# A spectral layer and an MLP on one core: MLP parts in a fixed order on TensorE, a stage moved to a later stretch, constants split early

## The chip, the cores and the metric

The kernel runs on one core of a Trainium2 chip. A core has TensorE (PE: matmuls, with its weight loads shown apart as PEld), VectorE (DVE), ScalarE (ACT), GpSimd (POOL) and SyncE (SP, which only issues DMAs here). ACT issues some DMAs too. The metric is the device time of one execution in microseconds; less is better.

## The reference

An input `x` of 8 batches, 3008 rows and 256 columns goes through a Fourier transform along the rows, a complex linear map with a soft threshold, and the inverse transform. The 24064 resulting rows are the tokens of an MLP with 2048 hidden units.

```python
X = np.fft.rfft(x, axis=1)
Yr = Xr @ w_r - Xi @ w_i + b_r
Yi = Xr @ w_i + Xi @ w_r + b_i
Yr = np.sign(Yr) * np.maximum(np.abs(Yr) - lam, 0.0)      # Yi likewise, lam = 0.01
y = np.fft.irfft(Y, n=x.shape[1], axis=1)
h = y.reshape(B * S, D) @ w_in
out = np.maximum(0.01 * h, h) @ w_out
```

## The kernel before

**The transform** of length 3008 = 47 x 64 is done in stages, each a set of matmuls. `fwd(b)`, the first stage of batch b, loads `xin`, folds it on POOL (`fold`), splits it into a high and a low half on DVE (`split`), multiplies it with `fa` (PE, L78, `psf<-xz,fa`), copies the result on ACT (L256) and stores it to `u_dram`. `mid(b)`, the middle stage, takes 12 pairs of columns one after the other: it loads `u` from `u_dram` (SP, L321), multiplies with `fb` (`stage_b`, PE L335), splits the result into `eh` (ACT and DVE, L346 to L351), multiplies with `wr`, `wn` and `wd` (`proj`, PE L78), applies the threshold (DVE L382 to L384), splits again into `zh`, multiplies with `gb` (`stage_g`) and stores `v_dram`. `inverse` (PE L472) and `forms` make the tokens of a chunk of 512: `yh` and `yl`, the high and low halves of seven sums of blocks. Products are taken in high and low halves throughout, three matmuls for one product.

**The MLP** works on 47 chunks of tokens with 8 steps each, 376 steps in all. A step does two of the 16 blocks of hidden units as a 2 x 2 block product by seven products (a scheme of Strassen's kind). `moe_a` issues four of them, twelve matmuls of 256 columns (PE L84, `psh<-yh,win`), into two PSUM banks b1 and b2; then ACT copies a quarter out (`p1`, L534) and DVE makes three sums of 256 columns that read the banks: `u2` (L535), and two into `gf` (L537, L538). `moe_b` adds the other three products, nine matmuls, to the same quarters of the banks: first b1, then b2. Its results go through ACT (L548), DVE (L549, 512 columns) and ACT (L551) into `gf`, then through ACT into `gh` (L553, 1024 columns) and DVE into `gl = gf - gh` (L555, 1024 columns). `moe_o` multiplies `gh` and `gl` with `wout`, six matmuls of 512 columns (PE L568) for each half of the output, LAG = 2 steps later. There are four `psh` banks, so two steps are in flight.

**What sets the order.** The code is written as generators: `moe()` yields twice in each step, and at each yield a share of the other stages' work is taken from a `Stream`, in proportion to how far the MLP has come. The time of the MLP is cut into stretches by `read[b]`, the point at which batch b's tokens are first needed. In stretch `cur` the streams are `fwd(cur + 2)` and `mid(cur + 1)`. From this a scheduler in the framework fixes, for each engine, the order of the instructions before the program runs; it picks by priority and by what its own timing of the program says is ready. At run time each engine then takes its instructions in that order. `tc.issue_after(ins)` puts the instructions that are traced within it behind `ins`, on `ins`'s engine alone, and adds no wait.

`split_consts` splits six constants into halves (ACT casts the high half, DVE subtracts for the low half). It is called after `mid(0)` behind a DVE instruction of it.

Of the kernel before, what the change touches and what calls it, by code (L numbers as in the profile page):

```python
# [8 lines left out]
F32 = mybir.dt.float32  # L9
# [21 lines left out]
def spectral_mlp_kernel(  # L31
# [16 lines left out]
    nc = tc.nc  # L48
    NB = x.shape[0]
# [8 lines left out]
    CS = 512  # L58
    LAG = 2

    NPRE = 2
# [5 lines left out]
    sync, act, dve, pool = nc.sync, nc.scalar, nc.vector, nc.gpsimd  # L67

    def bank(tag, bufs):
        return ps.tile([P, 512], F32, name=tag, tag=tag, bufs=bufs)  # L70

    def products(dst, pairs):
# [5 lines left out]
            last = nc.tensor.matmul(dst, a, b, start=(i == 0), stop=(i == len(terms) - 1))  # L78
        return last

    def block(dst, l, r, start=False):

        for i, (a, b) in enumerate(((l[0], r[0]), (l[0], r[1]), (l[1], r[0]))):
            nc.tensor.matmul(dst, a, b, start=start and i == 0, stop=i == 2, skip_group_check=True)  # L84

    def flat(t):
        return t.rearrange("p a b -> p (a b)")
# [4 lines left out]
    def pair(name, shape):  # L92
        consts[name] = tuple(const.tile(shape, F32R, name=f"{name}_{p}") for p in ("hi", "lo"))
        return consts[name]
# [5 lines left out]
    def split_consts():  # L100
        for name in ("wr", "wd", "wn", "gb", "fa0", "fa1"):
            w = consts[name + "32"][0]
            hi, lo = pair(name, list(w.shape))
            act.copy(hi, w)
            dve.tensor_sub(lo, w, hi.bitcast(F32))
# [12 lines left out]
    def float64_parts(raw, a, q):  # L118


        wl, wh = raw[:, :, 0], raw[:, :, 1]
        u = a.bitcast(U32)
        act.mul(q, wl, 2.0 ** -52)
        act.activation(a, wh.bitcast(F32), AF.Abs, scale=2.0 ** 16)
        dve.tensor_scalar(a, a, F64_MIN * 2.0 ** 16, F64_MAX * 2.0 ** 16, ALU.max, ALU.min)
        dve.tensor_scalar(u, u, 4, 1, ALU.logical_shift_left, ALU.logical_shift_right)
        dve.scalar_tensor_tensor(u, wh, 0x80000000, u, ALU.bitwise_and, ALU.bitwise_or)
        dve.tensor_scalar(wl, u, 0xFF800000, None, ALU.bitwise_and)
        dve.tensor_mul(q, q, wl.bitcast(F32))


    made, converted = [], []


    NIN = DF // 4
# [13 lines left out]
    def convert_win(c):  # L149


        a, q, s = win_tmp
        float64_parts(win_raw[c], a, q)
        dve.tensor_add(a, a, q)
        a = a.rearrange("p (j q i m) -> p j q i m", j=NH, q=2, i=2)
        a11, a12, a21, a22 = (a[:, j, :, i] for i in range(2) for j in range(2))
        dve.tensor_add(s[:, 0], a21, a22)
        dve.tensor_sub(s[:, 2], a11, a21)
        dve.tensor_sub(s[:, 1], s[:, 0], a11)
        dve.tensor_sub(s[:, 3], a12, s[:, 1])  # L160
        hi, lo = (w[:, :, 2 * c:2 * c + 2] for w in consts["win"])
        for k, w in ((slice(0, 2), a[:, :, :, 0]), (2, a22), (slice(3, 7), s)):
            act.copy(hi[:, k], w)
            last = dve.tensor_sub(lo[:, k], w, hi[:, k].bitcast(F32))
        return last
# [37 lines left out]
    reads, written, turned, turning, thresholded = [], [], [], [], []  # L203
# [100 lines left out]
    def mid(b):  # L304
# [13 lines left out]
        def load(j):  # L318
            u = sb.tile([P, 2, D], F32, name="u", tag="u", bufs=3)
            for c in range(2):  # L320
                ld = sync.dma_start(u[c * N2:(c + 1) * N2], ud[c, 2 * j:2 * j + 2, :N2, :].rearrange("k n d -> n k d"))  # L321
                if b == 0:
                    reads.append(ld)
            u_t[j] = u
# [88 lines left out]

        for j in range(2):
            load(j)
        yield 0
        if b:
            for s in range(NPAIR):
                if s + 2 < NPAIR:
# [100 lines left out]
    def product(dst, ci, q, k, start=False):  # L520
        block(
            dst, tuple(w[:, AK[k - 1], q] for w in consts["win"]), tuple(y[:, BK[k - 1]] for y in y_t[ci]), start)

    def moe_a(ci, q):

        b1, b2 = bank("psh", 4), bank("psh", 4)
        lo, hi = slice(0, HT), slice(HT, NT)
        product(b1[:, lo], ci, q, 1, True)
        product(b1[:, hi], ci, q, 6)
        product(b2[:, hi], ci, q, 7, True)  # L530
        product(b2[:, lo], ci, q, 5)
        p1 = sb.tile([P, HT], F32, name="p1", tag="p1", bufs=1)
        u2 = sb.tile([P, HT], F32, name="u2", tag="u2")
        act.copy(p1, b1[:, lo])  # L534
        dve.tensor_add(u2, b1[:, hi], p1)  # L535
        g = sb.tile([P, 4, HT], F32, name="gf", tag="gf")
        dve.tensor_add(g[:, 3], b2[:, hi], u2)  # L537
        dve.tensor_add(g[:, 3], b2[:, lo], g[:, 3])  # L538
        h_t[ci, q] = (b1, b2, u2, g)

    def moe_b(ci, q):

        b1, b2, u2, g = h_t.pop((ci, q))
        lo, hi = slice(0, HT), slice(HT, NT)
        product(b1[:, lo], ci, q, 2)
        product(b2[:, lo], ci, q, 3)
        product(b2[:, hi], ci, q, 4)
        act.activation(g[:, 0], b1[:, lo], AF.Prelu, alpha=SLOPE)  # L548
        dve.tensor_add(  # L549
            g[:, 1:3], b2.rearrange("p (k n) -> p k n", k=2), u2.unsqueeze(1).broadcast_to([P, 2, HT]))  # L550
        act.activation(g[:, 1:4], g[:, 1:4], AF.Prelu, alpha=SLOPE)  # L551
        gh = sb.tile([P, 4, HT], F32R, name="gh", tag="gh")
        act.copy(gh, g)  # L553
        gl = sb.tile([P, 4, HT], F32R, name="gl", tag="gl")
        dve.tensor_sub(gl, g, gh.bitcast(F32))  # L555
        g_t[ci, q] = (gh, gl)

    def moe_o(ci, q, eh):
        gh, gl = (t.rearrange("p (i k) n -> p i (k n)", i=2) for t in g_t[ci, q])
        wh, wl = consts["wout"]  # L560
        if q == 0:
            o_t[ci, eh] = bank("pso", 2)
        po = o_t[ci, eh]
        s = slice(eh * P, (eh + 1) * P)
        for i in range(2):
            f = 2 * q + i
            for j, (a, r) in enumerate(((wh, gh), (wl, gh), (wh, gl))):
                nc.tensor.matmul(  # L568
                    po, a[:, f, s], r[:, i], start=(f == 0 and j == 0), stop=(f == NF - 1 and j == 2),
                )  # L570
        if q == NQ - 1:
            ob = sb.tile([P, NT], F32, name="ob", tag="y")
            act.copy(ob, po)
            sync.dma_start(out[s, ci * NT:(ci + 1) * NT], ob)

    steps = [(ci, q) for ci in range(nch) for q in range(NQ)]
# [22 lines left out]
    def moe():  # L599

        for i, (ci, q) in enumerate(steps):
            if q == 0:
                nxt = tokens(ci + 1) if ci + 1 < nch else iter(())
            moe_a(ci, q)
            if i >= LAG:
                moe_o(*steps[i - LAG], 0)
            next(nxt, None)
            yield ci + (q + 0.5) / NQ
            if i >= LAG:
                moe_o(*steps[i - LAG], 1)  # L610
            moe_b(ci, q)
            next(nxt, None)
            if q == NQ - 1:
                for _ in nxt:
                    pass
            yield ci + (q + 1) / NQ
        for s in steps[-LAG:]:
            for eh in range(NH):
                moe_o(*s, eh)

    class Stream:
        def __init__(self, gen, total):
# [13 lines left out]
    MID = NPAIR * (16 * P + 18 * D + 3 * CS)  # L636
    FWD = NS * 6 * D
# [33 lines left out]
    dve.tensor_sub(bz[32:33], brow[32:33], bz[32:33].bitcast(F32))  # L671
    act.mul(fa32[:, 2], fa32[:, 1], -1.0)
    convert_win(0)
    m0 = Stream(mid(0), MID)
    m0.to(0.001)
    for c in range(2, 4):
# [22 lines left out]
    for eh in range(NH):  # L699
        for p in due[0]:  # L700
            inverse(p, eh)
    with tc.issue_after(thresholded[-1].ins):
        split_consts()
    for _ in forms(0):
        pass
    next(wout)
    next(wout)


    mids = [Stream(mid(b), MID) for b in range(1, NB)]  # L710
    cur, streams = -1, ()
    for i, pos in enumerate(moe()):
        if i % 2 == 0 and len(converted) < NQ:
            with tc.issue_after(made[0].ins):
                next(wout, None)
        if i in (2, 4):
            with tc.issue_after(made[0].ins):
                next(fp.gen)
        while cur + 1 < NB - 1 and pos >= (read[cur + 1] if cur >= 0 else 0):
            for s in streams:  # L720
                s.finish()
            cur += 1
            streams = ([Stream(fwd(cur + NPRE), FWD)] if cur + NPRE < NB else []) + [mids[cur]]
        frac = (pos - read[cur]) / (read[cur + 1] - read[cur]) if cur + 1 < NB else 1
        if cur == 0:
            frac = max(0, frac - 0.2) * 1.25
        work = frac / 0.95 * sum(s.total for s in streams)
        with tc.issue_after(converted[-1].ins) if cur == 0 else nullcontext():
            for s in streams:
                s.to(work / s.total)  # L730
                work = max(0, work - s.total)
# [103 lines left out]
```

## Time and profile before

| | |
|---|---|
| median of 3 runs | 2608.39 us (2605.04 to 2613.94) |
| the profiled execution: time, span of its instructions | 2609.83 us, 2608.0 us |
| PE busy | 2543.3 us, 98% of the span, 16300 matmuls |
| PEld busy | 2283.9 us, 88% |
| DVE busy | 1884.8 us, 72% |
| ACT busy | 1654.5 us, 63% |
| POOL busy | 248.2 us, 10% |
| granted TensorE clock, mean | 0.991 |
| chain that ended last | PE 90%, DVE 3%, ACT 3%, DMA 1% |

Busy times are unions of the instructions' spans. Matmuls overlap, so what PE has room for is read from the distance between the starts of neighbouring matmuls, not from the duration of one. In the tables of stretches, each engine has its busy time and, in brackets, the number of its instructions.

### The profile page before, as it was taken

What the parts mean: (1) busy time and instruction counts of PE and PEld (TensorE: products, weight loads), DVE (VectorE), ACT (ScalarE), POOL (GpSimd) and SP (SyncE); (2) the same over time, 40 slices, a digit from 0 to 9 for tenths busy, and PEclk for the clock granted to TensorE, in tenths of its full rate; (3) what the DMA queues carried; (4) which work ended last, traced back from release to release, by engine and by line L of the source; (5) the groups of instructions that cost most, each with busy time, mean ns of one, the idle gap of its engine ahead of it and who ended that gap; (6) DMA issues with size and microseconds to landing.
All of it is one profiled execution on the core that took longest, in us unless ns stands there. A gap on an engine that the chain in (4) does not pass through costs nothing.

```text
span 2608.0 us, 42647 instructions
## 1 busy us (share of the span) xinstructions
PE 2543.3 (98%) x16300; PEld 2283.9 (88%) x16300; DVE 1884.8 (72%) x3403; ACT 1654.5 (63%) x3174; POOL 248.2 (10%) x180
## 2 busy tenths in 40 slices
PE   5899999999999999999999999999999999999999
PEld 3678887999989999899999999999999999989998
DVE  6697667777787777777777777777777767667665
ACT  4665665676656666567665766666666666655554
POOL 0002102100120001200021000211000000000000
PEclk8999999999999999999999999999999999999999
DMA  8634113211142112312123111231111111100000
GB/s 248 172 99 116 53 42 92 84 52 47 32 120 61 48 37 56 101 53 59 33 74 94 52 45 41 74 94 52 45 41 53 41 41 44 42 18 32 9 17 17
DMA packets 119914, 165.14 MB, mean 63 GB/s; under 512 B 13602, under 2 KB 69918, under 8 KB 119710
## 3 DMA queue, kind: packets, MB, share of 16 engines
q1 hardware_dynamic: 79120, 115.55, 14.5%
q10 hardware_dynamic: 40589, 46.87, 7.1%
q8 instruction: 128, 2.10, 0.3%
q14 instruction: 77, 0.62, 0.1%
HBM read 86.60 MB, written 75.76 MB: 62 GB/s over the span
## 4 chain that ended last, share of the span: by engine, by line
PE 90%; DVE 3%; ACT 3%; DMA 1%; issue 1%; ACTq 0%; SPq 0%; DVEq 0%
PE pso L568 38%; PE psh L84 34%; PE psf L78 11%; PE psf L472 3%; PE psf L335 3%; DVE gl L555 1%; ACT zf L392 0%; ACT gh L553 0%; ACT gf L551 0%; DMA u_dram<-xin 0%; DVE yl L498 0%; ACT zf L388 0%; DMA raw<-w_out_dram 0%; DVE gf L549 0%; ACTq L412 0%
## 5 line engine op out<-in xcount | busy, mean ns | idle before, releaser
L84 PE MATMUL psh<-yh,win_hi 128*128 128x256 f32 x2632 | 738.4, 285 | 8.1 <-ACT yh L497 4.1
L84 PE MATMUL psh<-yl,win_hi 128*128 128x256 f32 x2632 | 735.1, 281 | 0.0
L84 PE MATMUL psh<-yh,win_lo 128*128 128x256 f32 x2632 | 727.2, 280 | 0.0
L555 DVE TENSOR_TENSOR gl<-gf,gh 128x1024 fp32r<-128x1024 f32 x376 | 475.9, 1266 | 197.5 <-ACT gh L553 195.9
L568 PE MATMUL pso<-gh,wout_hi 128*128 128x512 f32 x1504 | 596.0, 396 | 1.9 <-ACT gh L553 1.8
L568 PE MATMUL pso<-gh,wout_lo 128*128 128x512 f32 x1504 | 591.3, 393 | 0.0
L568 PE MATMUL pso<-gl,wout_hi 128*128 128x512 f32 x1504 | 559.8, 396 | 2.7 <-DVE gl L555 2.4
L84 PEld LDWEIGHTS psh<-yh,win_hi 128*128 128x128 f32 x2632 | 494.3, 189 | 33.6 <-ACT yh L497 5.7
L84 PEld LDWEIGHTS psh<-yl,win_hi 128*128 128x128 f32 x2632 | 497.1, 189 | 25.8 <-issue 0.5
L84 PEld LDWEIGHTS psh<-yh,win_lo 128*128 128x128 f32 x2632 | 493.5, 189 | 4.0 <-issue 0.2
L551 ACT ACTIVATE gf<-gf 128x768 f32<-128x768 f32 x376 | 318.6, 848 | 216.3 <-DVE gf L549 211.3
L553 ACT CAST gh<-gf 128x1024 fp32r<-128x1024 f32 x376 | 395.5, 1052 | 16.5 <-ACT gf L551 10.5
L549 DVE TENSOR_TENSOR gf<-psh,u 128x512 f32<-128x512 f32 x376 | 258.9, 689 | 198.4 <-PE psh L84 196.6
L568 PEld LDWEIGHTS pso<-gl,wout_hi 128*128 128x128 f32 x1504 | 282.5, 188 | 60.7 <-DVE gl L555 7.9
L568 PEld LDWEIGHTS pso<-gh,wout_lo 128*128 128x128 f32 x1504 | 282.9, 188 | 45.1
L568 PEld LDWEIGHTS pso<-gh,wout_hi 128*128 128x128 f32 x1504 | 283.0, 188 | 41.2 <-ACT gh L553 3.0
L548 ACT ACTIVATE gf<-psh 128x256 f32<-128x256 f32 x376 | 144.4, 384 | 214.2 <-PE psh L84 193.0
L371 POOL TENSOR_TENSOR kb<-bias,kc 128x512 f32<-128x512 f32 x84 | 121.4, 1446 | 1468.3 <-ACT kc L368 1302.2
L534 ACT COPY p<-psh 128x256 f32<-128x256 f32 x376 | 139.5, 371 | 100.0 <-PE psh L84 82.2
L535 DVE TENSOR_TENSOR u<-psh,p 128x256 f32<-128x256 f32 x376 | 157.8, 420 | 60.8 <-ACT p L534 58.2
L537 DVE TENSOR_TENSOR gf<-psh,u 128x256 f32<-128x256 f32 x376 | 157.6, 420 | 22.3 <-PE psh L84 11.1
L538 DVE TENSOR_TENSOR gf<-psh,gf 128x256 f32<-128x256 f32 x376 | 158.0, 421 | 6.8
(134 smaller groups left out, 3290.9 us busy)
## 6 DMA issues: line engine op xcount, KB each, us to landing
u<-u_dram SPq DMA_DIRECT2D x192, 128.0 KB, 2.7
v_dram<-v ACTq DMA_DIRECT2D x192, 128.0 KB, 2.4
out_dram<-ob SPq DMA_DIRECT2D x94, 256.0 KB, 2.1
vin<-v_dram SPq DMA_DIRECT2D x96, 240.0 KB, 3.5
xin<-x_dram SPq DMA_DIRECT2D x90, 240.0 KB, 3.0
u_dram<-xin ACTq DMA_DIRECT2D x72, 240.0 KB, 2.4
u_dram<-xin SPq DMA_DIRECT2D x24, 240.0 KB, 4.6
raw<-w_out_dram SPq DMA_DIRECT2D x8, 512.0 KB, 4.9
```

The source lines that it names most:

```text
L78: last = nc.tensor.matmul(dst, a, b, start=(i == 0), stop=(i == len(terms) - 1))
L84: nc.tensor.matmul(dst, a, b, start=start and i == 0, stop=i == 2, skip_group_check=True)
L534: act.copy(p1, b1[:, lo])
L535: dve.tensor_add(u2, b1[:, hi], p1)
L537: dve.tensor_add(g[:, 3], b2[:, hi], u2)
L538: dve.tensor_add(g[:, 3], b2[:, lo], g[:, 3])
L548: act.activation(g[:, 0], b1[:, lo], AF.Prelu, alpha=SLOPE)
L549: dve.tensor_add(g[:, 1:3], b2.rearrange("p (k n) -> p k n", k=2), u2.unsqueeze(1).broadcast_to([P, 2, HT]))
L551: act.activation(g[:, 1:4], g[:, 1:4], AF.Prelu, alpha=SLOPE)
L553: act.copy(gh, g)
L555: dve.tensor_sub(gl, g, gh.bitcast(F32))
L568: nc.tensor.matmul(po, a[:, f, s], r[:, i], start=(f == 0 and j == 0), stop=(f == NF - 1 and j == 2),)
```

## The change

It has three parts.

1. `in_order` puts each part of the MLP on PE behind the last matmul of the part before. The order of the parts in a step is also another: it was first products, output half 0, output half 1, last products in the code (with the scheduler free to mix them); it is now first products (of step i), output half 0 (of step i - 2), last products (of step i), output half 1 (of step i - 2), and the scheduler can't mix them any more. Other stages' matmuls may still stand between them.
2. `fwd(b)` for b from 2 to 7 is taken in stretch b - 1, ahead of `mid(b)` in the same stretch, where it was taken in stretch b - 2 beside `mid(b - 1)`. The middle stage yields 6 * CS of work after its first loads, so that its first matmul comes about a step later in the order. The two last pieces of `fwd(1)` stand behind `gh` and `gl` of the first steps.
3. `split_consts` is called after the first stage of batch 0, with its ACT halves behind the last copy of that stage; its DVE halves are no longer behind `mid(0)`.

```diff
+    mlp = []
+    def in_order(part, *args):
+        with tc.issue_after(mlp[0].ins) if mlp else nullcontext():
+            part(*args)
...
-            nc.tensor.matmul(dst, a, b, start=start and i == 0, stop=i == 2, skip_group_check=True)
+            mlp[:] = [nc.tensor.matmul(dst, a, b, start=start and i == 0, stop=i == 2, skip_group_check=True)]
...
-        yield 0
+        yield 6 * CS if b else 0
...
-        dve.tensor_sub(gl, g, gh.bitcast(F32))
+        parted[:] = [cp, dve.tensor_sub(gl, g, gh.bitcast(F32))]
...
-            moe_a(ci, q)
+            in_order(moe_a, ci, q)
             if i >= LAG:
-                moe_o(*steps[i - LAG], 0)
+                in_order(moe_o, *steps[i - LAG], 0)
             next(nxt, None)
             yield ci + (q + 0.5) / NQ
+            in_order(moe_b, ci, q)
             if i >= LAG:
-                moe_o(*steps[i - LAG], 1)
-            moe_b(ci, q)
+                in_order(moe_o, *steps[i - LAG], 1)
...
+    with tc.issue_after(turned[0].ins):
+        split_consts()
...
-    with tc.issue_after(thresholded[-1].ins):
-        split_consts()
...
-    mids = [Stream(mid(b), MID) for b in range(1, NB)]
+    mids = [Stream(mid(b), MID + 6 * CS) for b in range(1, NB)]
...
-            with tc.issue_after(made[0].ins):
+            with tc.issue_after(parted[0].ins), tc.issue_after(parted[1].ins):
                 next(fp.gen)
...
-            streams = ([Stream(fwd(cur + NPRE), FWD)] if cur + NPRE < NB else []) + [mids[cur]]
+            streams = ([Stream(fwd(cur + 1), FWD + 4 * CS)] if cur else []) + [mids[cur]]
```

What stands where is seen best at the end of the program, where no other stage's work is left. The names carry buffer numbers; all lines of the changed kernel's MLP are 8 higher (L84 is L92, L568 is L576, L535 is L543, L537 and L538 are L545 and L546, L549 is L557, L555 is L563). First PE before, from the last of the first products of one step (banks `psh_28039` and `psh_28040`) on:

```order
L84 MATMUL psh_28040<-yh_27478,win_lo_187 128x256
L84 MATMUL psh_27991<-yh_27478,win_hi_186 128x256
L84 MATMUL psh_27991<-yl_27479,win_hi_186 128x256
L84 MATMUL psh_27991<-yh_27478,win_lo_187 128x256
L84 MATMUL psh_27991<-yh_27478,win_hi_186 128x256
L84 MATMUL psh_27991<-yl_27479,win_hi_186 128x256
L84 MATMUL psh_27991<-yh_27478,win_lo_187 128x256
L84 MATMUL psh_28039<-yh_27478,win_hi_186 128x256
L84 MATMUL psh_28039<-yl_27479,win_hi_186 128x256
L84 MATMUL psh_28039<-yh_27478,win_lo_187 128x256
L568 MATMUL pso_27813<-gh_27986,wout_hi_897 128x512
L568 MATMUL pso_27813<-gh_27986,wout_lo_898 128x512
```

Ten more matmuls of L568 follow before `psh_28040` is written again. The same banks on PE in the changed kernel:

```order
L92 MATMUL psh_28040<-yh_27478,win_lo_187 128x256
L576 MATMUL pso_27813<-gh_27980,wout_hi_897 128x512
L576 MATMUL pso_27813<-gh_27980,wout_lo_898 128x512
L576 MATMUL pso_27813<-gl_27982,wout_hi_897 128x512
L576 MATMUL pso_27813<-gh_27980,wout_hi_897 128x512
L576 MATMUL pso_27813<-gh_27980,wout_lo_898 128x512
L576 MATMUL pso_27813<-gl_27982,wout_hi_897 128x512
L92 MATMUL psh_28039<-yh_27478,win_hi_186 128x256
L92 MATMUL psh_28039<-yl_27479,win_hi_186 128x256
L92 MATMUL psh_28039<-yh_27478,win_lo_187 128x256
L92 MATMUL psh_28040<-yh_27478,win_hi_186 128x256
```

Before, six matmuls of 256 columns on `psh_27991`, three on `psh_28039` and twelve of 512 columns stand between the last first product and the return to `psh_28040`; now six of 512 and three of 256. DVE at the same place before (`gf_27959` and `gf_28008` are the results of two neighbouring steps, and `gl_27988` is made from `gf_27959`):

```order
L535 TENSOR_TENSOR u2_28005<-psh_27990,p1_28004 128x256
L549 TENSOR_TENSOR gf_27959<-psh_27942,u2_27956 128x512
L537 TENSOR_TENSOR gf_28008<-psh_27991,u2_28005 128x256
L538 TENSOR_TENSOR gf_28008<-psh_27991,gf_28008 128x256
L535 TENSOR_TENSOR u2_28054<-psh_28039,p1_28053 128x256
L555 TENSOR_TENSOR gl_27988<-gf_27959,gh_27986 128x1024
L537 TENSOR_TENSOR gf_28057<-psh_28040,u2_28054 128x256
L538 TENSOR_TENSOR gf_28057<-psh_28040,gf_28057 128x256
```

DVE now, the same two steps:

```order
L557 TENSOR_TENSOR gf_27959<-psh_27942,u2_27956 128x512
L563 TENSOR_TENSOR gl_27982<-gf_27959,gh_27980 128x1024
L543 TENSOR_TENSOR u2_28005<-psh_27990,p1_28004 128x256
L545 TENSOR_TENSOR gf_28008<-psh_27991,u2_28005 128x256
L546 TENSOR_TENSOR gf_28008<-psh_27991,gf_28008 128x256
L557 TENSOR_TENSOR gf_28008<-psh_27991,u2_28005 128x512
L563 TENSOR_TENSOR gl_28031<-gf_28008,gh_28029 128x1024
```

Before, `gl` of one step stood behind all three reads (L535, L537, L538) of the next step's banks; now it stands ahead of them. In the middle of the program, where other stages' work stands between, an example on DVE now, from `gl` of one step to the last read of the next step's banks:

```order
L563 TENSOR_TENSOR gl_13249<-gf_13207,gh_13247 128x1024
L509 TENSOR_TENSOR yt_13411<-yc_12722 128x256
L543 TENSOR_TENSOR u2_13275<-psh_13260,p1_13274 128x256
L484 TENSOR_TENSOR y_13376<-psf_13370,odd_13375 128x240
L486 TENSOR_TENSOR y_13376<-psf_13370,odd_13375 128x230
L545 TENSOR_TENSOR gf_13278<-psh_13261,u2_13275 128x256
L390 TENSOR_TENSOR t_13423<-psf_13382,kb_13297 128x512
L511 TENSOR_TENSOR yt_13411<-yc_12722,yt_13411 128x256
L512 TENSOR_TENSOR yc_12722<-yc_12722 128x256
L546 TENSOR_TENSOR gf_13278<-psh_13261,gf_13278 128x256
```

Six instructions of other stages stand between `gl` and L546 here; in the kernel before, L538 of the same numbered step follows L537 directly, with no other stage's work behind `gl`:

```order
L538 TENSOR_TENSOR gf_13399<-psh_13382,gf_13399 128x256
L555 TENSOR_TENSOR gl_13360<-gf_13312,gh_13358 128x1024
L535 TENSOR_TENSOR u2_13462<-psh_13447,p1_13461 128x256
L537 TENSOR_TENSOR gf_13465<-psh_13448,u2_13462 128x256
L538 TENSOR_TENSOR gf_13465<-psh_13448,gf_13465 128x256
```

That `gl` belongs to the step two before, not to the step just before.

More of the change, by code (lines that the diff above doesn't have):

```diff
@@ L129, in float64_parts @@
         dve.tensor_mul(q, q, wl.bitcast(F32))
-    made, converted = [], []
+    made, converted, parted = [], [], []
     NIN = DF // 4
@@ L552, in moe_b @@
         gh = sb.tile([P, 4, HT], F32R, name="gh", tag="gh")
-        act.copy(gh, g)
+        cp = act.copy(gh, g)
         gl = sb.tile([P, 4, HT], F32R, name="gl", tag="gl")
-        dve.tensor_sub(gl, g, gh.bitcast(F32))
+        parted[:] = [cp, dve.tensor_sub(gl, g, gh.bitcast(F32))]
         g_t[ci, q] = (gh, gl)
@@ L567, in moe_o @@
             for j, (a, r) in enumerate(((wh, gh), (wl, gh), (wh, gl))):
-                nc.tensor.matmul(
+                mlp[:] = [nc.tensor.matmul(
                     po, a[:, f, s], r[:, i], start=(f == 0 and j == 0), stop=(f == NF - 1 and j == 2),
-                )
+                )]
         if q == NQ - 1:
@@ L618, in moe @@
             for eh in range(NH):
-                moe_o(*s, eh)
+                in_order(moe_o, *s, eh)
     class Stream:
```

## The prediction

> **What bounds the kernel now.** I read the table of stretches first, since a mean of 98% for PE can hide a stage. Columns: stretch, its length, busy time and (instructions) of PE, PEld, DVE, ACT, POOL, then the granted clock, DMA share and GB/s.
>
> ```profile
> 140.00:160.00 20.00, 17.53 (x115) 15.29 (x113) 17.45 (x38) 13.73 (x29) 0.00 (x0) 1.00 0.32 102
> 200.00:300.00 100.00, 96.21 (x602) 85.73 (x601) 71.61 (x127) 59.93 (x113) 20.44 (x14) 0.98 0.29 82
> 300.00:400.00 100.00, 89.18 (x584) 81.11 (x582) 66.70 (x126) 66.57 (x140) 9.34 (x8) 0.95 0.19 53
> 400.00:500.00 100.00, 95.03 (x572) 83.55 (x573) 76.29 (x129) 55.61 (x109) 22.78 (x16) 0.97 0.34 99
> 500.00:600.00 100.00, 100.00 (x676) 91.99 (x675) 78.69 (x146) 70.38 (x143) 9.57 (x6) 1.00 0.19 53
> ...
> 230.00:240.00 10.00, 8.29 (x40) 6.24 (x38) 6.42 (x9) 4.22 (x7) 5.08 (x4) 1.00 0.36 98
> 240.00:250.00 10.00, 7.92 (x43) 6.78 (x44) 8.25 (x21) 7.09 (x17) 0.00 (x0) 0.83 0.65 189
> 2300.00:2600.00 300.00, 299.76 (x1909) 270.16 (x1908) 195.98 (x348) 167.31 (x294) 0.00 (x0) 1.00 0.05 18
> ```
>
> From 500 us to the end PE is full and at full clock, so nothing can be gained there; all a new order can do there is lose. Between 200 and 500 us, the first stretch, PE idles 3.79 + 10.82 + 4.97 = 19.6 us, and the clock of 0.98, 0.95 and 0.97 costs another 2 + 5 + 3 = 10 us. The chain of waits says the same (what waited, for whom, us in total, times, longest): first PE's waits from 200 to 500 us, then from 500 to 2580 us.
>
> ```profile
> PE psf L78 <- DVE xz L246: 5.1, 4, 2.4
> PE psh L84 <- ACT yh L497: 4.1, 2, 3.6
> PE psf L78 <- DVE yt L503: 4.0, 1, 4.0
> ...
> PE pso L568 <- DVE gl L555: 0.7, 1, 0.7
> ```
>
> The `xz` waits are the first stage of batch 2, which leaves this stretch. After 500 us the longest sum is 0.7 us.
>
> **The new wait, from the rows of one step.** The end of the program has no other stage's work, so the latencies stand there bare (start us, us, engine, line).
>
> ```profile
> 2597.68 0.28 PE L84 MATMUL psh<-yl,win_hi 128*128 128x256 f32 x1
> 2597.80 0.27 PE L84 MATMUL psh<-yh,win_lo 128*128 128x256 f32 x1
> 2597.91 0.40 PE L568 MATMUL pso<-gh,wout_hi 128*128 128x512 f32 x1
> 2598.15 0.39 PE L568 MATMUL pso<-gh,wout_lo 128*128 128x512 f32 x1
> ...
> 2588.91 0.69 DVE L549 TENSOR_TENSOR gf<-psh,u 128x512 f32<-128x512 f32 x1 [0.45 <-PE psh L84]
> 2589.52 0.41 DVE L537 TENSOR_TENSOR gf<-psh,u 128x256 f32<-128x256 f32 x1
> 2589.97 0.42 DVE L538 TENSOR_TENSOR gf<-psh,gf 128x256 f32<-128x256 f32 x1
> 2594.03 0.42 DVE L538 TENSOR_TENSOR gf<-psh,gf 128x256 f32<-128x256 f32 x1
> 2594.37 0.68 DVE L549 TENSOR_TENSOR gf<-psh,u 128x512 f32<-128x512 f32 x1
> 2597.05 1.23 DVE L555 TENSOR_TENSOR gl<-gf,gh 128x1024 fp32r<-128x1024 f32 x1 [2.00 <-ACT gh L553]
> 2598.19 0.68 DVE L549 TENSOR_TENSOR gf<-psh,u 128x512 f32<-128x512 f32 x1
> 2600.87 1.23 DVE L555 TENSOR_TENSOR gl<-gf,gh 128x1024 fp32r<-128x1024 f32 x1 [1.99 <-ACT gh L553]
> ...
> 2598.91 0.85 ACT L551 ACTIVATE gf<-gf 128x768 f32<-128x768 f32 x1 [1.89 <-DVE gf L549]
> 2599.79 1.05 ACT L553 CAST gh<-gf 128x1024 fp32r<-128x1024 f32 x1
> ...
> 2602.15 0.50 PE L568 MATMUL pso<-gl,wout_hi 128*128 128x512 f32 x1
> ```
>
> Counted from the start of a step's last `moe_b` matmul (2597.80, 0.27 long): L549 can start 0.05 after its end, at +0.33 (here it started a little later, since DVE was at `gl` until then). From there by the rows L551 follows after 0.72, L553 after 0.88 and L555 (`gl`) after 1.08, at +3.01. In the changed order DVE has the next step's L535, L537 and L538 behind this `gl`, so it stands waiting for `gh` and can't make them earlier. L535 follows `gl` after 1.14 (2597.05 to 2598.19), L537 and L538 after 0.45 each (2589.52 to 2589.97), L538 takes 0.42, and PE starts 0.05 after its releaser (2600.87 + 1.23 to 2602.15): 3.01 + 1.14 + 0.45 + 0.45 + 0.42 + 0.05 = 5.52 us until PE may write bank b2 again.
>
> PE's cover for this, in the new order: the last matmul 0.117, one output half of six at 0.23 (1.39), the next step's twelve first products at 0.117 (1.40), the other output half (1.39), and three matmuls on b1 (0.35) = 4.64 us. So a bare step waits 5.52 - 4.64 = 0.88 us, and since the next step's chain starts from PE's delayed matmul, nothing of it is made up. Before, `gl` stood behind these reads and the cover was another output half and more; hence the 0.7 us above.
>
> **The sum over the steps.** I counted, in the changed order, what stands between these instructions in each of the 375 pairs of neighbouring steps. In 240, `gl` is ahead of all three reads, in 117 between them, in 18 behind. PE's cover is longer where other stages' matmuls stand in it (up to 8.3 us), and the chain is longer where other stages' work stands in DVE's or ACT's way. An inserted DVE instruction counts 0.34 (256 columns, 2594.03 to 2594.37) or 0.61 (512 columns, 2588.91 to 2589.52), one on ACT about 0.5. The example in the part on the change has three of 256, two of 240 and 230, one of 512 behind `gl` (2.2 us) and one copy on ACT ahead of `gh` (0.6): chain 5.5 + 2.2 + 0.6 = 8.3, cover 6.9, wait 1.4.
> - Bare chain against each step's cover: 131 steps wait, 95 us. This is the low end: it holds if all inserted work finds room.
> - With the DVE work behind `gl` and ahead of L538: 162 us.
> - With the ACT work between L551 and `gh` too: 200 us. An engine takes its instructions in order, so these delays are certain in kind; I take this.
> - With work that stands earlier, as far as it outlasts the idle time there (1.99 us before `gl`): 275 us, the high end, since some of it is there before it is needed.
>
> The same count over the order before gives 0, 0 and 3 us for the first three, against 0.7 us of such waits seen.
>
> **First stretch.** At best all 30 us of 200 to 500 us come back; at worst nothing, since `mid(1)` and the waits on `yh` stay. The waits of its MLP steps are counted anew above (27 of the 200), so I take the 30.
>
> **Constants.** DVE halves on the path before, then the place where DVE and ACT have room:
>
> ```profile
> 103.89 0.69 DVE L384 TENSOR_TENSOR t<-t,c 128x512 f32<-128x512 f32 x1
> 104.50 0.69 DVE L105 TENSOR_TENSOR wr_lo<-w,wr_hi 128x512 fp32r<-128x512 f32 x1
> ...
> 106.99 0.71 DVE L390 TENSOR_SCALAR zf<-t,sign 64x256 f32<-64x256 f32 x2
> ...
> PE psh L78 <- DVE zf L390: 4.4, 1, 4.4
> ...
> 39.07 0.69 DVE L125 TENSOR_SCALAR cva<-cva 128x1024 f32<-128x1024 f32 x1 [5.65 <-ACT cva L124]
> ```
>
> PE waits 4.4 us for `zf`, and six subtractions stand ahead of it: 106.99 - 104.58 = 2.4 us gained. They now stand where DVE is idle for 5.65 us, which covers them, and the ACT halves go behind the last `xin` copy, ahead of casts that wait for DVE: nothing.
>
> **Stage A moved.** Its PE, DVE, POOL and DMA work is the same, one stretch later; POOL at 10% and DMAs hide it. But `mid(b)` now reads what `fwd(b)` has just stored.
>
> ```profile
> u<-u_dram SPq DMA_DIRECT2D x192, 128.0 KB, 2.7
> u_dram<-xin ACTq DMA_DIRECT2D x72, 240.0 KB, 2.4
> ...
> L256 ACT COPY xin<-psf 120x256 f32<-120x256 f32 x12 | 4.5, 376 | 2.9 <-issue 1.6 <-PE psf L78 1.2
> ...
> L321 SPq DMA_DIRECT2D u<-u_dram x192: 573/583/1405, 37.9 to 2153.9; - x192
> ```
>
> Matmul 0.28, copy 0.38, store 2.4, two issues of 0.58 ahead of the third load, load 2.7, four hand-overs of 0.05: 7.1 us. In the new order 5.0 to 5.35 us of PE work stand between, and about 1 us of waits from above: 0 to 2 us at six places, 0 to 12. I take 6. Behind these loads on SP wait two stores of `out_dram`, whose buffers are needed later than that.
>
> In 14 places PE has the first `proj` matmul only 0.35 us behind its `stage_b`; one such place gave the 4.0 us wait on `yt` above. They lie in steps that wait about 2 to 3 us for L538 anyway, at the same time, so they add 0 to (4.0 - 0.35 - 2.1) x 14 = 22 us; I take 0, as both waits run together. The two last pieces of `fwd(1)` move a few us; `mid(1)` needs them some 60 us later: nothing.
>
> **Sum.** 2608.0 - 30 - 2.4 + 200 + 6 = 2782 us of span. The profiled execution took 2609.83, 1.8 more than its span, and the median is 1.4 below it, so 2782 stands for the median too.
>
> **Rivals.**
> - *Only the bare steps wait.* Inserted work fits into DVE's 1.99 us idle before `gl`. For it: DVE is busy 65% even in the bare stretch (195.98 of 300). Against: work behind `gl` can't use the idle time ahead of it. 2608 - 32 + 95 + 6 = 2677 us. Chance 0.16.
> - *No slower.* If the chain from `moe_b` to L538 closed within 4.64 us, only the gains stayed: 2576 us. It decides where the mean wait of a step falls under 32/375 = 0.09 us, that is where the chain is 0.8 us shorter than its rows. Against: the rows are a clean run of that very chain, with ACT and DVE idle before L551 and L555. Chance 0.07.
> - *The clock falls with the many short waits.* In 230 to 240 us PE idled 17% and the clock fell to 0.83 in the next 10 us; a bare step would now idle 0.88 of 6.1, 14%. At 0.83 throughout, PE's 2438 us after 140 us (2608 - 140 - 30) become 2937, 3077 in all; but PE's cover grows to 5.59 then, the wait goes, the clock returns, so about half way: 2930 us. Against: 140 to 160 us idled 12% at clock 1.00. Chance 0.07. [...]
>
> **How the numbers follow.** Forecast 0.70. Range: low end 2608 - 32 + 95 = 2671, high end 2608 - 2 + 275 + 22 + 12 = 2915; so 2670 to 2915; it takes in the first rival and leaves out the second and the third. Measured times here tell 0.3% (8 us) from no change. Faster 0.05, same 0.02 (both of the second rival), slower 0.93.
>
> **What would show it.** PE busy far below 98%, its waits `psh L92 <- DVE gf L546` some 200 us in sum, 0.9 us each in the last 300 us; DVE idle before `gl`, ended by `gh`; PE's span from 200 to 500 us without `xz` waits; `zf` some 2 us earlier near 107 us; clock 1.00. It is wrong if those waits are under 100 us in sum, or if the clock is below 0.97 after 500 us.

## The result, and the profile after

The changed kernel takes 2907.89 us (median of 4 runs, 2903.71 to 2913.01) against 2607.77 for the kernel before on the same chip (4 runs): ratio 1.1148, 95% interval 1.1121 to 1.1175. It is 300 us slower; the forecast was 174 slower, 2782 us, and its range, to 2915, holds it at its upper end. The profiled execution took 2913.01 us, its span is 2911.2.

The stretches first (PE, PEld, DVE, ACT, POOL busy, granted clock, DMA share, GB/s):

```profile
200.00:300.00 100.00, 92.58 (x590) 82.76 (x589) 65.74 (x123) 61.85 (x125) 8.61 (x5) 0.97 0.17 47
300.00:400.00 100.00, 93.66 (x594) 82.96 (x593) 68.44 (x120) 61.76 (x121) 16.93 (x12) 0.98 0.21 58
400.00:500.00 100.00, 92.63 (x559) 80.50 (x559) 69.08 (x126) 56.68 (x107) 12.85 (x10) 0.98 0.28 79
500.00:600.00 100.00, 93.83 (x591) 82.44 (x590) 64.62 (x119) 60.68 (x119) 6.38 (x4) 0.98 0.16 45
...
2300.00:2600.00 300.00, 282.39 (x1750) 245.31 (x1749) 186.06 (x335) 170.64 (x323) 13.07 (x9) 0.99 0.12 34
```

PE now idles 6 to 7% in every stretch shown, in those that were full before too; 200 to 500 us, which was to gain 30 us, is no better than it was. Next, what PE waited for over the whole span (us in total, times, longest):

```profile
PE psh L92 <- DVE gf L546: 84.0, 166, 3.2
PE psh L92 <- DVE u L543: 39.3, 123, 3.2
...
PE psf L78 <- ACT eh L358: 16.2, 10, 2.5
PE psf L78 <- DVE xz L254: 11.5, 24, 1.8
```

The first row is the wait that was forecast; before, the longest sum of waits after 500 us was 0.7. The second is the same wait one bank earlier (b1 instead of b2). The other two are waits of other stages. Third, the page's group of `gl` (busy, mean ns, idle time of DVE just before it and who ended it), before and after:

```profile
L555 DVE TENSOR_TENSOR gl<-gf,gh 128x1024 fp32r<-128x1024 f32 x376 | 475.9, 1266 | 197.5 <-ACT gh L553 195.9
L563 DVE TENSOR_TENSOR gl<-gf,gh 128x1024 fp32r<-128x1024 f32 x376 | 466.1, 1240 | 448.7 <-ACT gh L561 444.4
```

DVE now stands 449 us before `gl`, waiting for `gh`, where it stood 198. How PE's time is lost by that, a bare step shows. It has no other stage's work; these are its rows on PE, DVE and ACT from one `gl` to the next, in order of time (start us, us):

```profile
2694.40 1.23 DVE L563 TENSOR_TENSOR gl<-gf,gh 128x1024 fp32r<-128x1024 f32 x1 [2.00 <-ACT gh L561]
...
2697.70 0.28 PE L92 MATMUL psh<-yh,win_lo 128*128 128x256 f32 x1
...
2698.01 0.69 DVE L557 TENSOR_TENSOR gf<-psh,u 128x512 f32<-128x512 f32 x1 [1.07 <-PE psh L92]
...
2698.74 0.84 ACT L559 ACTIVATE gf<-gf 128x768 f32<-128x768 f32 x1 [1.69 <-DVE gf L557]
2699.61 1.05 ACT L561 CAST gh<-gf 128x1024 fp32r<-128x1024 f32 x1
...
2700.70 1.23 DVE L563 TENSOR_TENSOR gl<-gf,gh 128x1024 fp32r<-128x1024 f32 x1 [2.00 <-ACT gh L561]
2701.84 0.42 DVE L543 TENSOR_TENSOR u<-psh,p 128x256 f32<-128x256 f32 x1
2702.36 0.42 DVE L545 TENSOR_TENSOR gf<-psh,u 128x256 f32<-128x256 f32 x1
2702.82 0.42 DVE L546 TENSOR_TENSOR gf<-psh,gf 128x256 f32<-128x256 f32 x1
...
2703.30 0.39 PE L92 MATMUL psh<-yh,win_hi 128*128 128x256 f32 x1 [0.37 <-DVE gf L546]
2703.53 0.28 PE L92 MATMUL psh<-yl,win_hi 128*128 128x256 f32 x1
```

From the last `moe_b` matmul (2697.70) `gl` follows after 3.00 us and PE's return to b2 (2703.30) after 5.60; forecast were 3.01 and 5.52. A step takes 2700.70 - 2694.40 = 6.30 us, where its 21 matmuls of 256 and 12 of 512 columns at 0.117 and 0.231 need 5.23. So it loses 1.07 us, against 0.88 forecast. The 0.08 of the longer chain and the 0.11 by which the first matmul after the wait is longer (2703.30 to 2703.53 is 0.23 instead of 0.12) make up the difference.

For the whole kernel I worked out, from the trace, the distance from each matmul's start to the next one's, took off the distance at full speed (0.231, 0.118, 0.101 us for 512, 256, 128 columns) and put what was left down to the releaser of the later matmul. Half clock is what the distances grew while the granted clock was at half. The sums from 140 us to the end, in us, for the kernels of this study (the runs are told below; e6, not in the table, sums to 51):

| | bank waits (`u2`, `gf`) | first matmul after a wait | other stages' waits | half clock | waits on `gh`, `gl` | rest | sum |
|---|---|---|---|---|---|---|---|
| before | 3 | 3 | 14 | 7 | 7 | 19 | 53 |
| changed | 178 | 44 | 85 | 32 | 0 | 16 | 355 |
| e1, part 1 alone | 196 | 47 | 67 | 27 | 0 | 14 | 351 |
| e2, parts 2 and 3 | 3 | 7 | 5 | 2 | 17 | 13 | 47 |
| e3, old order fixed | 17 | 4 | 13 | 3 | 1 | 9 | 47 |
| e4, `gl` behind the reads | 63 | 20 | 21 | 3 | 0 | 15 | 122 |
| e5, `gh` and `gl` behind | 33 | 9 | 14 | 3 | 0 | 13 | 72 |
| e7, old order, `gl` first | 309 | 51 | 95 | 61 | 1 | 14 | 531 |
| e8, free, then held | 3 | 4 | 5 | 0 | 5 | 12 | 29 |

### The profile page after: what moved, and what is told of

Its sections match the earlier page's. It is cut to its first block, busy times and chain, and to the rows that moved or that the text cites. A ratio compares the mean times of both kernels' runs of the same rounds, so it can differ in the third digit from the quotient of the medians.

```text
span 2911.2 us, 43056 instructions
## 1 busy us (share of the span) xinstructions
PE 2685.1 (92%) x16300; PEld 2313.2 (79%) x16300; DVE 1896.7 (65%) x3403; ACT 1671.0 (57%) x3174; POOL 241.1 (8%) x180
## 4 chain that ended last, share of the span: by engine, by line
PE 43%; DVE 27%; ACT 18%; issue 4%; POOL 1%; DMA 1%; DVEq 0%; ACTq 0%; POOLq 0%; SPq 0%
PE psh L92 18%; PE pso L576 16%; DVE gl L563 7%; PE psf L78 7%; ACT gh L561 6%; ACT gf L559 5%; DVE gf L557 4%; DVE gf L545 3%; DVE gf L546 3%; DVE u L543 2%; PE psf L480 2%; PE psf L343 2%; ACT zf L400 1%; ACT zf L396 1%; DVE yl L506 1%
## 5 line engine op out<-in xcount | busy, mean ns | idle before, releaser
L92 PE MATMUL psh<-yh,win_hi 128*128 128x256 f32 x2632 | 792.3, 301 | 124.6 <-DVE gf L546 84.0
L563 DVE TENSOR_TENSOR gl<-gf,gh 128x1024 fp32r<-128x1024 f32 x376 | 466.1, 1240 | 448.7 <-ACT gh L561 444.4
L92 PE MATMUL psh<-yl,win_hi 128*128 128x256 f32 x2632 | 741.6, 282 | 0.1
L92 PE MATMUL psh<-yh,win_lo 128*128 128x256 f32 x2632 | 740.0, 281 | 0.0
L92 PEld LDWEIGHTS psh<-yh,win_hi 128*128 128x128 f32 x2632 | 500.4, 190 | 246.8 <-DVE gf L546 129.0
L576 PE MATMUL pso<-gh,wout_lo 128*128 128x512 f32 x1504 | 598.1, 398 | 0.0
L576 PE MATMUL pso<-gh,wout_hi 128*128 128x512 f32 x1504 | 598.0, 398 | 0.0
L576 PE MATMUL pso<-gl,wout_hi 128*128 128x512 f32 x1504 | 595.7, 396 | 0.0
L92 PEld LDWEIGHTS psh<-yl,win_hi 128*128 128x128 f32 x2632 | 501.2, 190 | 23.3 <-DVE yl L506 0.3
L92 PEld LDWEIGHTS psh<-yh,win_lo 128*128 128x128 f32 x2632 | 500.1, 190 | 0.1
L557 DVE TENSOR_TENSOR gf<-psh,u 128x512 f32<-128x512 f32 x376 | 258.4, 687 | 206.1 <-PE psh L92 205.7
L576 PEld LDWEIGHTS pso<-gl,wout_hi 128*128 128x128 f32 x1504 | 286.4, 190 | 65.6 <-DVE wout_lo L202 0.2
L576 PEld LDWEIGHTS pso<-gh,wout_hi 128*128 128x128 f32 x1504 | 287.0, 191 | 35.5 <-issue 0.2
L576 PEld LDWEIGHTS pso<-gh,wout_lo 128*128 128x128 f32 x1504 | 286.4, 190 | 32.1
L379 POOL TENSOR_TENSOR kb<-bias,kc 128x512 f32<-128x512 f32 x84 | 127.3, 1515 | 1714.0 <-ACT kc L376 1624.7
L543 DVE TENSOR_TENSOR u<-psh,p 128x256 f32<-128x256 f32 x376 | 157.1, 418 | 93.4 <-ACT p L542 93.3
L545 DVE TENSOR_TENSOR gf<-psh,u 128x256 f32<-128x256 f32 x376 | 158.7, 422 | 28.9 <-PE psf L78 0.5
L546 DVE TENSOR_TENSOR gf<-psh,gf 128x256 f32<-128x256 f32 x376 | 157.8, 420 | 6.1
```

What stands on the lines that cost most here:

```text
L92: mlp[:] = [nc.tensor.matmul(dst, a, b, start=start and i == 0, stop=i == 2, skip_group_check=True)]
L557: dve.tensor_add(g[:, 1:3], b2.rearrange("p (k n) -> p k n", k=2), u2.unsqueeze(1).broadcast_to([P, 2, HT]))
L563: parted[:] = [cp, dve.tensor_sub(gl, g, gh.bitcast(F32))]
L576: mlp[:] = [nc.tensor.matmul(po, a[:, f, s], r[:, i], start=(f == 0 and j == 0), stop=(f == NF - 1 and j == 2),)]
```

## The experiments

Two theories stood against each other in most of them. Theory G: all of the loss comes from `gl` standing ahead of the reads on DVE, which the fixed new order brought about. Against it, in turn: that parts 2 and 3 make a share of it, that a fixed order costs by itself, and that PE's place of the last products makes the wait. Counted in the traces, `gl` stands ahead of all three reads of the next step in 17 of the 375 pairs of steps before, in 240 in the changed kernel, and from e1 to e8 in 245, 7, 5, 0, 0, 13, 375 and 7.

**e1: part 1 alone, on the kernel before** (`in_order` and `mlp` as in the change).

```diff
-            moe_a(ci, q)
+            in_order(moe_a, ci, q)
             if i >= LAG:
-                moe_o(*steps[i - LAG], 0)
+                in_order(moe_o, *steps[i - LAG], 0)
...
+            in_order(moe_b, ci, q)
             if i >= LAG:
-                moe_o(*steps[i - LAG], 1)
-            moe_b(ci, q)
+                in_order(moe_o, *steps[i - LAG], 1)
```

> The kernel before with part 1 alone: the new code order, each MLP part on PE behind the one before; fwd stays two stretches ahead and the constants are split late. In its order gl stands ahead of all three reads of the next step's banks in 245 of 375 pairs of steps, between them in 109, behind in 21, nearly as in the changed kernel (240, 117, 18). Theory G (the whole loss is made by the gate chain, and what shows as other waits and half clock comes with the fixed order too): 2608 + 190 (the same count of chain against cover) + 60 to 100 = 2860 to 2900 us, waits on gf L545 and u2 L542 of 110 us and more. Rival S (the part of the loss above the forecast comes from fwd and mid standing in one stretch): 2608 + 190 to 210 = 2800 to 2820 us, and hardly any wait of PE on xz or eh after 500 us.

Measured: 2905.24 us, ratio 1.1128 (1.1110 to 1.1147). Part 1 alone makes the whole loss, a little more than either theory had said. PE's waits over the span (lines are one lower than in the changed kernel):

```profile
PE psh L91 <- DVE gf L545: 94.4, 184, 3.3
PE psh L91 <- DVE u L542: 41.6, 141, 3.0
...
PE psf L78 <- ACT eh L357: 14.1, 8, 2.7
PE psf L78 <- DVE xz L253: 10.8, 28, 1.8
```

The waits on `eh` and `xz` are there without part 2, after 500 us too (10.6 and 8.4 us of them), so Rival S falls.

**e2: the changed kernel without part 1.**

```diff
-            in_order(moe_a, ci, q)
+            moe_a(ci, q)
...
-            in_order(moe_b, ci, q)
             if i >= LAG:
-                in_order(moe_o, *steps[i - LAG], 1)
+                moe_o(*steps[i - LAG], 1)
+            moe_b(ci, q)
```

> The changed kernel without part 1: the old code order and the scheduler free to mix the MLP parts; fwd in the stretch of its own mid, constants early. gl stands behind all three reads in 275 of 375 pairs. Theory G: the forecast's gains without its loss, 2608 - 30 - 2 + 6 = 2580 us, at worst 2605 if the first stretch gives nothing. Rival S: xz, eh and yc waits of some 70 us stay, 2640 to 2680 us.

Measured: 2599.53 us, ratio 0.9964 (0.9951 to 0.9977), a small gain. Its stretches:

```profile
200.00:300.00 100.00, 99.30 (x666) 90.56 (x665) 72.33 (x135) 66.80 (x138) 10.72 (x7) 1.00 0.18 48
300.00:400.00 100.00, 99.98 (x657) 90.78 (x657) 73.14 (x129) 65.09 (x127) 16.17 (x12) 1.00 0.22 62
400.00:500.00 100.00, 97.54 (x623) 86.89 (x622) 76.44 (x139) 63.20 (x126) 14.43 (x11) 1.00 0.31 87
```

The first stretch is now nearly full and at full clock: from 140 to 500 us the account loses 13 us where the kernel before lost 40, so the 27 us are real. But 16 of the 27 are lost again after 2320 us (17 us against 1.5), in waits on `gh` and `gl` for the most part: the free scheduler places the MLP's parts differently there. Why parts 2 and 3 bring that about was not looked into. In its waits from 2300 us on stands

```profile
PE pso L576 <- ACT gh L561: 5.9, 18, 2.6
```

**e3: fixed, but in the old order.**

```diff
-            in_order(moe_b, ci, q)
             if i >= LAG:
                 in_order(moe_o, *steps[i - LAG], 1)
+            in_order(moe_b, ci, q)
```

> The changed kernel with each MLP part still held behind the one before, but in the old code order: first products, both output halves, last products. PE's cover between a step's last product and the return to b2 is then the next step's first products and two output halves again, and the scheduler puts gl behind all reads in 313 of 375 pairs; chain against cover gives 4 to 5 us. Theory G (the place of the last products, not the fixing, makes the wait): 2585 to 2625 us. Rival F (fixing costs by itself, since PE can't take another part while one waits): waits of PE on the MLP's banks and on gh stay above 100 us, 2720 us and more.

Measured: 2602.44 us, ratio 0.9977 (0.9968 to 0.9987). Rival F falls: holding each part behind the one before costs next to nothing in itself. Why the old order differs can be counted out from bare rows; the scheduler's own timing, by which it chose, was not looked at. From the last `moe_b` matmul to the return to b2 PE has the same matmuls in either order (twelve first products, two output halves of six, three on b1), 4.5 us in bare steps. But in the old order the first products come straight behind `moe_b`, so their results are there some 1.4 us after it, long before `gh` (3.0 us), and the reads stand ahead of `gl`. In the new order an output half stands between, the results are there after 2.8 us, and `gl` goes first. So the longer cover that the prediction named for the kernel before is not what keeps the wait away: here it is the same, and the order on DVE and ACT differs.

**e4: the changed kernel with `gl` held behind the next step's reads.**

```diff
+        read2 = dve.tensor_add(g[:, 3], b2[:, lo], g[:, 3])
+        if late:
+            moe_gl(read2)
...
+    def moe_gl(behind=None):
+        ci, q, g, gh, cp = late.pop()
         gl = sb.tile([P, 4, HT], F32R, name="gl", tag="gl")
-        parted[:] = [cp, dve.tensor_sub(gl, g, gh.bitcast(F32))]
+        with tc.issue_after(behind.ins) if behind is not None else nullcontext():
+            parted[:] = [cp, dve.tensor_sub(gl, g, gh.bitcast(F32))]
```

> The changed kernel with one DVE instruction a step moved: gl of a step is held behind the last read (gf, second sum) of the next step's bank b2. PE's order of the MLP parts stays as in the changed kernel. Theory G: the waits on u2 and gf lose gl (1.14 us) and the wait for gh ahead of it: from about 160 us in sum after 140 us to under 40; time 2620 to 2700 us. ACT still has gh ahead of p1 of the next step in 194 pairs: 3.0 + 0.4 + 3 x 0.45 = 4.75 us against a cover of 4.64, so a rest of 0.1 us and what is inserted stays there. Rival C (short pauses and half clock come from the order on PE, whoever makes them wait): 2800 us and more.

Measured: 2681.10 us, ratio 1.0274 (1.0258 to 1.0289). One DVE instruction a step, moved behind three others, takes away 227 of the 300 us, with the order of the MLP's matmuls on PE unchanged in the trace. Rival C falls. PE's waits (lines two higher than in the changed kernel at this place):

```profile
PE psh L92 <- DVE gf L548: 32.8, 52, 2.5
...
PE psh L92 <- DVE u L545: 11.4, 22, 2.1
...
PE psf L78 <- ACT eh L358: 6.1, 8, 2.4
```

The first two sum to 44 us, a little over the 40 that were expected. The other stages' waits and the half clock go with the bank waits (85 to 21 us and 32 to 3 us in the account), though nothing of those stages was moved by hand. The scheduler did move some of it, so the bare steps are the cleaner test; there `gl` now follows `gl` after 5.44 us instead of 6.30:

```profile
2648.64 1.22 DVE L572 TENSOR_TENSOR gl<-gf,gh 128x1024 fp32r<-128x1024 f32 x1
2654.08 1.22 DVE L572 TENSOR_TENSOR gl<-gf,gh 128x1024 fp32r<-128x1024 f32 x1
```

**e5: `gh` held back too**, behind `p1` on ACT, with `gl` as in e4.

```diff
+        copied = act.copy(p1, b1[:, lo])
...
+        summed = dve.tensor_add(g[:, 3], b2[:, lo], g[:, 3])
+        if late:
+            moe_split(copied, summed)
```

> The changed kernel with gh and gl of a step held behind the next step's reads: gh behind the copy p1 on ACT, gl behind the second gf sum on DVE; PE's order of the MLP parts as in the changed kernel. Theory G (what is left of the wait with gl alone moved, 34 us of gf and 13 of u2 in the waits, comes from gh standing ahead of p1 on ACT): those two fall to under 10 us together and the time to 2600 to 2625 us. Rival C (a rest comes from PE's fixed order itself): they stay at 40 us, 2670 to 2690 us.

Measured: 2628.86 us, ratio 1.0078 (1.0062 to 1.0095). Most of the rest of e4 was `gh` ahead of `p1`: after 2320 us, where little other work is left, the loss falls from 17 to 2 us. Over the whole span it did not fall as far as expected, neither the time nor these waits:

```profile
PE psh L92 <- DVE gf L548: 17.5, 33, 1.3
PE psh L92 <- DVE u L545: 7.4, 12, 1.9
```

25 us of waits are left, 23 of them before 2320 us, where other stages' work stands between the reads. I did not follow them further, so the last 26 us to the time of e3 stay open.

**e6: the new code order, nothing held.**

```diff
-            in_order(moe_b, ci, q)
+            moe_b(ci, q)
             if i >= LAG:
-                in_order(moe_o, *steps[i - LAG], 1)
+                moe_o(*steps[i - LAG], 1)
```

> The changed kernel with the new code order but the scheduler free to mix (nothing held behind anything in the MLP). gl stands behind all three reads in 280 of 375 pairs and the count of chain against cover gives 7 us. Theory G: as with parts 2 and 3 alone, 2590 to 2615 us. Rival O (the new code order alone brings the wait): 2700 us and more.

Measured: 2604.85 us, ratio 0.9985 (0.9976 to 0.9994). Rival O falls: the new code order harms only where the scheduler is held to it.

**e7: the old order on PE, but `gl` held ahead of the reads** (on the kernel of e3).

```diff
-        dve.tensor_add(u2, b1[:, hi], p1)
+        with tc.issue_after(parted[1].ins) if parted else nullcontext():
+            dve.tensor_add(u2, b1[:, hi], p1)
```

> The kernel of the run with the old order fixed (2602.4 us), with one order on DVE added: u2 of each step is held behind gl of the step before. PE's order of the MLP parts stays the old one, in which the wait was nearly absent. Theory G (the order on DVE makes the wait; PE's order only led the scheduler to it): gl is ahead of the reads in all 375 pairs; the count gives 285 us against 190 for the changed kernel, whose loss after 140 us is about 1.5 times its count: 2602 + 285 to 430 = 2890 to 3030 us. Rival P (PE's place of the last products makes the wait): within 40 us of 2602.

Measured: 3085.24 us, ratio 1.1832 (1.1814 to 1.1849). This turns e3 around with one order on DVE, +483 us:

```profile
PE psh L92 <- DVE u L544: 134.8, 200, 3.3
PE psh L92 <- DVE gf L547: 98.7, 219, 2.1
PE psf L78 <- ACT eh L358: 40.2, 20, 2.4
```

Most of the other stages' matmuls also came to stand at other places between the MLP's. The bare steps have none, and there `gl` follows `gl` after 5.23 us in e3 (first two rows) and 6.54 in e7:

```profile
2578.38 1.23 DVE L563 TENSOR_TENSOR gl<-gf,gh 128x1024 fp32r<-128x1024 f32 x1 [0.41 <-ACT gh L561]
2583.61 1.23 DVE L563 TENSOR_TENSOR gl<-gf,gh 128x1024 fp32r<-128x1024 f32 x1 [0.42 <-ACT gh L561]
...
3043.08 1.23 DVE L564 TENSOR_TENSOR gl<-gf,gh 128x1024 fp32r<-128x1024 f32 x1 [2.24 <-ACT gh L562]
3049.62 1.23 DVE L564 TENSOR_TENSOR gl<-gf,gh 128x1024 fp32r<-128x1024 f32 x1 [2.24 <-ACT gh L562]
```

On ACT, `gh` stands ahead of the next step's `p1` in none of e7's pairs (in 240 of the changed kernel's), so here `gl` makes the wait by itself. Rival P falls. The count of chain against cover said 285 us of bank waits; the account has 309 - 17 = 292. Even the upper end of what I expected in all was too low, since other stages' waits (+82) and half clock (+58) grew along.

**e8: parts 2 and 3, free, and held in the old order once no other stage's work is left.**

```diff
+        with tc.issue_after(mlp[0].ins) if held else nullcontext():
+            part(*args)
...
+            if ci + q / NQ >= read[-1]:
+                held[:] = [1]
```

> Parts 2 and 3 with the free order as in the run of 2599.5 us, and the MLP parts held in the old order from the point on where the last batch's tokens are first read, that is where no other stage's work is left. There the free order lost 17 us to gh and gl of the last steps (the kernel before: 1.5, the fixed old order: 0.5). Expected 2599.5 - 16 = 2584 us; if the held tail only moves the wait, 2595 to 2605 us.

Measured: 2583.01 us, ratio 0.9902 (0.9887 to 0.9917). It beats both kernels: the first stretch's gain stays, and the end is full again:

```profile
2300.00:2560.00 260.00, 260.00 (x1662) 234.95 (x1662) 175.61 (x301) 146.00 (x253) 0.00 (x0) 1.00 0.05 17
```

## Why the prediction was right in kind and 126 us short

Mechanism, direction and place were right. The place of `gl` on DVE made most of the loss (e4 and e7 move it by hand, both ways), that of `gh` on ACT most of the rest (e5), and the bare step's chain was 5.60 us against 5.52. Set side by side, the forecast has 174 us (-30 - 2.4 + 200 + 6) and the account 302 (175 bank waits, 41 first matmuls, 71 other stages' waits, 25 half clock, less 10 elsewhere). That the range still held the time is in part luck: its high end, 2915, stands on 275 us of waits for the reads, on 22 for `proj` and on 12 for first loads, and what filled the gap was other waits. Term by term:

- **Gate wait, +200.** The account has 178 - 3 = 175 us of bank waits, and 44 - 3 = 41 for the matmul that follows each (424 times about 0.10 us): 216 in all. By stretch the count had 27 us to 500 us and 173 after it; the bank waits are 22 and 156. That the two come so close is partly a matter of names, since some of the same chain's waits are booked under other stages (next point). The 0.10 us after each wait was no part of the count; it is lost only where no other wait follows at once, as b2's follows b1's in a bare step.
- **"PE's cover is longer where other stages' matmuls stand in it": this is the step that failed.** I counted what delays the three reads, and credited those matmuls as cover. I did not ask what those matmuls wait for. Some of them wait for DVE and ACT work that stands behind the same `gl` and `gh`. Three rows on DVE and two on PE of the changed kernel:

```profile
1858.83 1.21 DVE L563 TENSOR_TENSOR gl<-gf,gh 128x1024 fp32r<-128x1024 f32 x1
1859.96 0.41 DVE L254 CAST xz<-xin 120x512 fp32r<-120x512 f32 x1
1860.29 0.41 DVE L546 TENSOR_TENSOR gf<-psh,gf 128x256 f32<-128x256 f32 x1
...
1858.37 0.28 PE L92 MATMUL psh<-yh,win_lo 128*128 128x256 f32 x1
...
1860.42 0.49 PE L78 MATMUL psf<-xz,fa_hi 120*120 120x512 f32 x1 [1.78 <-DVE xz L254]
```

  The `xz` matmul stands between b1 and b2 on PE and was counted as cover for L546, but `xz` itself comes behind `gl`, so PE waits for it 1.78 us. Without it PE would have waited for L546, which ends at 1860.70: the wait only bears another name, and the matmul gave no cover. Waits of other stages sum to 85 us against 14 before: +71 where I had the 14 going away. After 2320 us, where few of those matmuls are left, they are 9 of 88 us, from 500 to 2320 us 60 of 212. Not each of them is shown to come straight from `gl` or `gh`: followed back in the trace after 500 us, through whatever released or preceded each instruction, some 26 us of them meet a `gl` or `gh` of the last 4 us before they meet PE. That they hang on the place of `gl` as a whole is what e4 shows (85 to 21). The 14 places of `stage_b` and `proj` that I took at 0 to 22 belong here.
- **First stretch, -30.** Right without part 1 (27 us in e2), wrong beside it: from 140 to 500 us the changed kernel loses 56 us, e1 without part 2 loses 54, e2 13. I read this as PE waiting for the MLP's own chain in any case, so that taking `xz` away gains nothing there. I added two terms that did not add.
- **Half clock.** Forecast 1.00 after 500 us; it was 0.99, and the account has 32 us against 7. The rival that would have taken it to 0.83 throughout did not come. Its 2930 us lies nearer to the measured time than the forecast, but by chance: half clock made 25 of the 300 us.
- **Transition, +6.** Waits of the middle stage on its loads of `u` in the changed kernel, after the first 140 us: 1.8 us in 2 places. In e3 they were 9.0 in 6.
- **Constants, -2.4.** PE's wait for `zf` near 107 us fell from 4.4 to 2.6 us as meant, but by the same account the first 140 us lost 75.0 us, and 70.6 in e2, against 74.0 and 73.1 in the two kernels without it (before and e1): a gain of 2 us can't be told from this.
- **The sign to look for.** I had named some 200 us of `psh L92 <- DVE gf L546`, and under 100 us as proof against. By the letter that row speaks against me: it has 84.0, and 123.3 with the row of `u2`. This view counts idle time only after the 0.28 us that a matmul is shown to last, though the next can start 0.117 after its start. I had set the sign in distances between starts; by those the two rows have 178 us.

Of the rivals, *only the bare steps wait* (2677) and *no slower* (2576) were far off; that inserted work adds to the chain was right.

## What to carry to other kernels

In a bare step `gl` waited 2.00 us for `gh`, with the next step's three reads behind it on DVE; held behind them instead, it made the step 5.44 us long where it was 6.30. Before matmuls of another stage are counted as cover for such a delay, look whether their own inputs come from behind that same instruction, as `xz` did here (1.78 us). A fixed order on one engine changes what the scheduler puts first on the others; read the order there, and mend it there (one instruction held back gave 227 of 300 us). A gain in waits and a new wait in the same stretch need not add: here the loss to 500 us was 56 us with the gain and 54 without it.

## What the runs showed of the hardware

**Where a weight load waited, it was 0.22 us from its matmul's start to the next one's, about 0.10 us more than elsewhere.** Weight loads (PEld) and matmuls at the return to b2 in the changed kernel:

```profile
2703.30 0.19 PEld L92 LDWEIGHTS psh<-yh,win_hi 128*128 128x128 f32 x1 [0.57 <-DVE gf L546]
2703.41 0.19 PEld L92 LDWEIGHTS psh<-yl,win_hi 128*128 128x128 f32 x1
```

The load starts at 2703.30 together with its matmul, and the next matmul starts 0.23 us later (2703.53); the next load starts 0.12 us ahead of its own matmul, as most loads that carry no wait do (median 0.116 us). In the kernel before and in the changed one it is the load that carries the wait (2988 and 2110 of 16300 loads, and no matmul). Each of the 391 matmuls before which PE stood idle over 0.15 us in the changed kernel has such a load, and it starts with the matmul or at most 0.03 us ahead, so there the weights are not loaded while PE waits. After 140 us, 313 of those matmuls have 256 columns; from their start to the next one's it is 0.223 us in the median, and 0.117 us where the load carries no wait. Whether a wait carried by the matmul would cost less, no run here shows.

**The clock fell after windows of 3.41 us in which PE idled about half or more.** Two pairs of neighbouring windows of the changed kernel, and one that had no effect (the clock is the third figure from the end):

```profile
591.49:594.90 3.41, 1.15 (x9) 0.90 (x8) 3.41 (x11) 2.98 (x8) 0.00 (x0) 0.99 0.26 77
594.90:598.31 3.41, 3.41 (x13) 2.93 (x12) 2.42 (x5) 1.25 (x3) 0.00 (x0) 0.51 0.13 30
1195.58:1198.99 3.41, 0.93 (x8) 0.72 (x8) 3.00 (x7) 3.14 (x8) 0.00 (x0) 1.00 0.27 77
1198.99:1202.40 3.41, 3.41 (x13) 3.02 (x14) 1.58 (x3) 0.42 (x1) 0.00 (x0) 0.50 0.00 0
1554.05:1557.46 3.41, 1.94 (x12) 1.80 (x13) 2.74 (x6) 1.40 (x4) 0.00 (x0) 1.00 0.26 77
1557.46:1560.87 3.41, 3.41 (x22) 3.03 (x22) 1.41 (x3) 2.17 (x3) 0.00 (x0) 1.00 0.00 0
```

Within each profile the half-clock stretches begin a whole number of 3.413 us apart. I laid that grid from 140 us on over the seven profiles that have such stretches well before their end (before, changed, e1, e3, e4, e5, e7). Of some 5160 full-clock windows in which PE idled under 1.3 us, none was followed by half clock; of 45 with 1.3 to 1.6 us, 8 were; of 80 with more, 77. So a wait shorter than a window was enough when enough of it fell in one: the first windows of the three pairs hold 2.26, 2.48 and 1.47 us of idle time, each from one wait for `eh` (2.27, 2.48 and 2.48 us), and the third of these waits began in the window before. Evenly spread short waits (1 us in each 6.3 us step) cost hardly any clock (0.99 in the last 300 us). Whether the limit is exactly half, and whether it is idle time or lost work that counts, these runs don't tell.
